# Taking seven more pairs of a gated MLP's hidden states down by block products, with their sums on VectorE

## The chip, the cores and the metric

One core of a Trainium2 chip runs the kernel. The metric is the device time of one execution in microseconds, the median over runs. Of the kernel before there are three runs.

## What is computed

All tensors are fp32. x has 2048 rows of 576. The result mixes two branches by a gate g:

```
g = sigmoid((x * gate_w).sum(-1))
a = linear attention with a softmax feature map on 32 heads of 18, then @ wo
gate, up = x @ W_gate, x @ W_up          # 576 x 4608 each
b = (gate * (gate > 0) * up) @ W_down    # 4608 x 576
out = g * a + (1 - g) * b
```

The attention branch and its projections are the first 350 us or so of the kernel. Everything in this document is about branch b, which is the rest.

## The kernel before

**Precision.** A matmul operand is kept as two parts of a narrower format, a high part (a rounding copy by ScalarE, `high`, `high_h`, `high_w`) and a low part (source minus high part, on VectorE: `low`, `low_h`, `low_w`, `low_w_rows`). A product of two blocks is then three matmuls of 128 x 128 by 512 columns: high x high, high x low, low x high.

**Units.** The 4608 hidden columns are 36 chunks of 128, the 2048 rows two halves of 1024. A unit is one chunk for one half: units 0 to 35 are the first half, 36 to 71 the second. `step(u, j)` (L1328) is one of seven steps j of a unit u. In each, TensorE runs one `product` (L1127), 7 matmuls, into a PSUM bank. The seven products are a block form (seven products where eight would be plain) of gate and up for two blocks of 512 rows. The bank `cx` takes four of them one on top of the other (steps 0, 2, 4 and 6), `ca` two (1 and 5), `cy` one (3). In between, a bank is read: ScalarE copies it out (`copy`, L1298: g1 from `cx` in step 1, u2 from `ca` in step 2, g2 from `cx` in step 3), VectorE adds to these copies (step 4: g1, step 5: u2 from `cx`, step 6: g2 from `ca`), and `gated` (L1295) makes the two hidden states, the second of them in step 0 of the next unit. The next product into a bank waits for the reading before it.

**Pairs.** Two units, 2g and 2g + 1, make pair g: four hidden states e1, e2, o1, o2 of 128 x 512. Pair g is taken down (multiplied by W_down, added to the output `ac` that stays in SBUF) during the two units of pair g + 1: behind each product stand some matmuls of the way down, whose sum VectorE adds to `ac` in the next step (`add_up`, L1279). There are 18 pairs a half (NG). Two ways down exist:
- `down_plain` (L1152), all pairs of the first half: eight blocks of 512 columns, each 6 matmuls and one add, and 8 matmuls for the last 64 of the 576 output columns, 56 matmuls and 8 adds. It needs 4 hidden states split in two and one split of the weights (`plain_down`, L1116).
- `down` (L1186), the second half's pairs but the last: fourteen block products of 3 matmuls and 8 for the last columns, 50 matmuls and 14 adds. It needs more sums: four differences of states (`minus`), 7 split states, and of each half of the weights four sums (`down_sums_of_blocks`, L1084, on GpSimd) and two splits (`prepare_down`, L1313).

**What else a unit does.** In the first half each unit also makes the next unit's gate and up operands from raw weights: high and low parts of three blocks (`blocks`, tile wb), four sums of blocks in place (`sums_of_blocks`, L891, VectorE), high and low parts of these (`block_sums`, tile ws). They are stored to DRAM, and the second half loads them. VectorE also works off 18 operations that prepare x for the second half (`second_half`, tile xb, one a unit from unit 4 on). Down weights come by `load_down` (L915) into one buffer.

**What sets the order.** `in_order` holds each engine's instructions in the order in which the program writes them, that of `step`. Engines meet through semaphores only. So an instruction that waits holds all that stands behind it on its engine. ScalarE's queue mixes the copies of banks with the high parts of states and weights.

Of the kernel before, what the change touches and what calls it, by code (L numbers as in the profile page):

```python
# [19 lines left out]
NC = F // P  # L20
# [63 lines left out]
def gated_mix_kernel(  # L84
# [26 lines left out]
    SUB, ADD, MULT = ALU.subtract, ALU.add, ALU.mult  # L111
    tt, pt = nc.vector.tensor_tensor, nc.gpsimd.tensor_tensor
# [98 lines left out]
    with tc.tile_pool(name="ps_v", bufs=1, space=PSUM) as ps_v:  # L211
# [7 lines left out]
        for k in range(5):  # L219
            w = raw.tile([P, TB + VW], F32, name="xwv", tag="raw")  # L220
# [438 lines left out]
    t = NT - 1  # L659
# [203 lines left out]
    NG = NC // 2  # L863
# [24 lines left out]
            WO[u] = {1: (o, 0), 2: (o, 1), 4: (o, 2)}  # L888
        f(WB[u], RAW[u][:, 0:3])

    def sums_of_blocks(u):  # L891

        a = RAW[u]
        f = tt
        f(out=a[:, 2], in0=a[:, 2], in1=a[:, 3], op=ADD)
        f(out=a[:, 3], in0=a[:, 0], in1=a[:, 3], op=SUB)
        f(out=a[:, 0], in0=a[:, 2], in1=a[:, 0], op=SUB)
        f(out=a[:, 1], in0=a[:, 1], in1=a[:, 0], op=SUB)

    def block_sums(u, f):  # L900
        if u not in WS:
# [163 lines left out]
    WD, W4, HID, ACC, ACC4, BANK, REST = {}, {}, {}, {}, {}, {}, {}  # L1065
# [17 lines left out]

    def down_sums_of_blocks(g, m):  # L1084
        a = down_raw(g, m)
        pt(out=a[:, 2], in0=a[:, 2], in1=a[:, 3], op=ADD)
        pt(out=a[:, 3], in0=a[:, 0], in1=a[:, 3], op=SUB)
        pt(out=a[:, 0], in0=a[:, 2], in1=a[:, 0], op=SUB)
        pt(out=a[:, 1], in0=a[:, 1], in1=a[:, 0], op=SUB)

    def down_block_sums(g, m, f):
        f(WD[g, m][:, :, 3:7], down_raw(g, m))
# [9 lines left out]
    def rest_weights(g, step):  # L1102

        a = WDR[g][:, 8 * P:].rearrange("p (c q) -> p c q", c=2)
        if step == 0:
            nc.scalar.activation(W4[g][:, 0:2, 0], a, AF.Copy)
        elif step == 1:
            tt(out=W4[g][:, 0:2, 1], in0=a, in1=W4[g][:, 0:2, 0].bitcast(F32), op=SUB)
            pt(out=a[:, 0], in0=a[:, 0], in1=a[:, 1], op=ADD)
        elif step == 2:  # L1110
            nc.scalar.activation(W4[g][:, 2, 0], a[:, 0], AF.Copy)
            nc.scalar.activation(W4[g][:, 3], W4[g][:, 1].bitcast(F32), AF.Copy, scale=-1.0)
        else:
            tt(out=W4[g][:, 2, 1], in0=a[:, 0], in1=W4[g][:, 2, 0].bitcast(F32), op=SUB)
# [29 lines left out]
    def load_rest(hf):  # L1144
        for t in range(2):
            a = ACC4[hf, t] = sums_of[t][:64, 2]
            nc.sync.dma_start(a, att[4 * P:, rows(0, 0, t, hf)[1]])

    PLAIN = {1: (0, 0, 1), 2: (0, 1, 1), 3: (2, 0, 1), 4: (0, 0, 0), 5: (0, 1, 0), 6: (2, 0, 0),
             8: (1, 0, 1), 9: (1, 1, 1), 11: (1, 0, 0), 12: (1, 1, 0)}  # L1150

    def down_plain(g, s):  # L1152
# [30 lines left out]
            return []  # L1183
        return add

    def down(g, s, bank):  # L1186

        first, last = g == NG, g == 2 * NG - 2
        m, i = divmod(s, 7)
        n = DOWN[i]  # L1190
        key = 0 if n in (1, 6, 7, 4) else 1
        if n in (1, 5, 2):
            BANK[m, key] = bank(m, n)
        ps = BANK[m, key]
        h, l = HID[g, n]
        o, k = WD[g, m], PLACE[n]
        mm = lambda ps, w, v, a, z: nc.tensor.matmul(ps, w, v, start=a, stop=z, skip_group_check=True)  # L1197
        mm(ps, o[:, 0, k], h, n in (1, 5, 2), False)
        mm(ps, o[:, 0, k], l, False, False)
        mm(ps, o[:, 1, k], h, False, True)  # L1200
        if m == 0 and n in (1, 5, 2, 4):
            w, r = {1: (0, 0), 5: (2, 1), 2: (1, 0), 4: (3, 1)}[n]
            if first and n in (1, 5):
                REST[r] = pm.tile([P, TB], F32, name=f"pm{r}")
            w = W4[g][:, w].rearrange("p s q -> p (s q)")
            mm(REST[r], w, h, first and n in (1, 5), False)
            mm(REST[r], w, l, False, last and n in (2, 4))

        def add():
            i, t = ADDS[n]  # L1210
            a = ACC[1, i, m, t]
            tt(out=a, in0=ps, in1=a, op=ADD)  # L1212
            return []
        return add
# [22 lines left out]
    def high_h(key, src):  # L1237
        h, l = hp.tile([P, TB], F32R, name="hh"), hp.tile([P, TB], F32R, name="hl")
        nc.scalar.activation(h, src, AF.Copy)  # L1239
        HID[key] = h, l  # L1240

    def low_h(key, src):
        h, l = HID[key]
        tt(out=l, in0=src, in1=h.bitcast(F32), op=SUB)  # L1244
# [29 lines left out]
    EVEN, ODD, T, LATE, PEND = {}, {}, {}, [], []  # L1274
# [16 lines left out]
    def minus(a, b):  # L1291

        tt(out=b, in0=a, in1=b, op=SUB)

    def gated(g, up):  # L1295
        nc.vector.scalar_tensor_tensor(out=g, in0=g, scalar=0.0, in1=up, op0=ALU.max, op1=MULT)  # L1296

    def copy(ps, name):  # L1298
        a = tp.tile([P, TB], F32, name=name, tag="tp")
        nc.scalar.activation(a, ps, AF.Copy)  # L1300
        return a
# [26 lines left out]
    def step(u, j):  # L1328


        g, odd = divmod(u, 2)
        v, q = u + 1, g - 1
        plain, was_plain = g < NG or g == 2 * NG - 1, q < NG
        ps, first = bank(SEQ[j])
        product(ps, u, SEQ[j], first)
        add_up()
        make = 0 < u < NC - 1
        cx, ca, cy = (BANKS.get(n) for n in ("cx", "ca", "cy"))
        old = not odd and g > 0

# [9 lines left out]
        if odd and plain or old and was_plain:  # L1350
            key, x2, x1 = ((g, 0), e2, e1) if odd else ((q, 1), o2, o1)
            if j == 0:
                high_h(key + (1,), x2)
            elif j == 1:
                high_h(key + (0,), x1)
                low_h(key + (1,), x2)
            elif j == 2:
                low_h(key + (0,), x1)
        elif odd:
            if j == 1:  # L1360
                high_h((g, 1), e1)
            elif j == 3:
                low_h((g, 1), e1)
                minus(e2, e1)
            elif j == 4:
                high_h((g, 5), e1)
            elif j == 5:
                low_h((g, 5), e1)
        elif old:
            if j == 0:  # L1370
                high_h((q, 6), e1)
                minus(o2, e2)
            elif j == 1:
                high_h((q, 3), o2)
                low_h((q, 6), e1)
            elif j == 2:
                low_h((q, 3), o2)
                high_h((q, 7), e2)
                high_h((q, 2), o1)
            elif j == 3:  # L1380
                minus(o1, e1)
                low_h((q, 7), e2)
            elif j == 4:
                high_h((q, 4), e1)
                low_h((q, 2), o1)
            elif j == 5:
                low_h((q, 4), e1)

        if make:
            if j == 0:  # L1390
                blocks(v, high_w)
                if v + 1 < NC:
                    load_w(v + 1)
            elif j == 1:
                blocks(v, low_w)
                blocks(v, low_w_rows)
            elif j == 2:
                if v < NC - 2:
                    nc.sync.dma_start(wbd[v], WB.pop(v).bitcast(F32))
                sums_of_blocks(v)  # L1400
            elif j == 4:
                if u > 1:
                    block_sums(v, low_w)
                    block_sums(v, low_w_rows)
            elif j == 5:
                if 2 < v < NC - 2:
                    nc.sync.dma_start(wsd[v], WS.pop(v).bitcast(F32))
        elif j == 0 and NC < u < 2 * NC - 1:
            load_operands(v)

        if j == 1:
            T["g1"] = copy(cx, "g1")
        elif j == 2:
            T["u2"] = copy(ca, "u2")
        elif j == 3:
            T["g2"] = copy(cx, "g2")
            if make:
                block_sums(v, high_w)
        elif j == 4:
            tt(out=T["g1"], in0=cy, in1=T["g1"], op=ADD)  # L1420
        elif j == 5:
            tt(out=T["u2"], in0=cx, in1=T["u2"], op=ADD)  # L1422
            if u == 1:
                block_sums(v, low_w)
                block_sums(v, low_w_rows)
                nc.sync.dma_start(wsd[v], WS.pop(v).bitcast(F32))
        elif j == 6:
            a = T["g2"]
            tt(out=a, in0=ca, in1=a, op=ADD)
            gated(a, T["u2"])  # L1430
            if odd and not plain:
                minus(a, e1)
            LATE[:] = [a, (cx, T["g1"])]
            w = WO.pop(u)
            if NC - 2 <= u < NC:
                WO[u + 2] = w
# [7 lines left out]
            prepare_down(g, 0, j)  # L1444
        elif old and not was_plain:
            prepare_down(q, 1, j)
        if old and j == 5:
            load_down(g)
        if old and j == 6:
            ODD.pop(q)  # L1450
# [28 lines left out]
                store_rest(0, 1)  # L1479
                load_rest(1)  # L1480
        if j == 6 and u < NC:
            if u >= 4:
                next(later_half, None)
            if u == NC - 3:
                for _ in later_half:
                    pass
                load_operand(1, 0)
                load_operand(1, 1)
# [157 lines left out]
```

## Time and profile before

| what | value |
|---|---|
| median of 3 runs | 1581.5 us (1580.53 to 1581.55) |
| the profiled execution | 1581.88 us, its span 1579.4 us |
| granted TensorE clock over the span | 1.000 |
| DMA | 283.38 MB, mean 179 GB/s |

The profile is of one execution. Its times count from the span's start. Engines are PE (TensorE), PEld (its weight loads), DVE (VectorE), ACT (ScalarE), POOL (GpSimd) and SP (the engine whose queue issues most DMAs). A record is an instruction's time on its engine; records of one engine can overlap a little, so the distance between two starts is what an instruction takes from the queue.

### The profile page before, as it was taken

What the parts mean: (1) busy time and instruction counts of PE and PEld (TensorE: products, weight loads), DVE (VectorE), ACT (ScalarE), POOL (GpSimd) and SP (SyncE); (2) the same over time, 40 slices, a digit from 0 to 9 for tenths busy, and PEclk for the clock granted to TensorE, in tenths of its full rate; (3) what the DMA queues carried; (4) which work ended last, traced back from release to release, by engine and by line L of the source; (5) the groups of instructions that cost most, each with busy time, mean ns of one, the idle gap of its engine ahead of it and who ended that gap; (6) DMA issues with size and microseconds to landing.
All of it is one profiled execution on the core that took longest, in us unless ns stands there. A gap on an engine that the chain in (4) does not pass through costs nothing.

```text
span 1579.4 us, 20181 instructions
## 1 busy us (share of the span) xinstructions
PE 1568.7 (99%) x7823; PEld 1313.6 (83%) x7823; DVE 1190.2 (75%) x1865; ACT 558.3 (35%) x918; POOL 175.7 (11%) x243
## 2 busy tenths in 40 slices
PE   9999999999999999999999999999999999999998
PEld 9999995678888888888888888888888888888887
DVE  4997776497787777877777777777777777777777
ACT  4354335563333333333333333232222332232321
POOL 0126521110000000000000002111111111111110
PEclk9999999999999999999999999999999999999999
DMA  5365415596755675555545516543443443443432
GB/s 165 105 202 186 167 33 154 180 359 265 257 201 199 221 277 207 192 222 214 196 176 210 220 43 231 196 177 132 158 179 132 166 156 132 179 157 132 186 136 75
DMA packets 64539, 283.38 MB, mean 179 GB/s; under 512 B 6802, under 2 KB 17298, under 8 KB 55740
## 3 DMA queue, kind: packets, MB, share of 16 engines
q1 hardware_dynamic: 61228, 270.34, 47.0%
q0 software_dynamic: 2352, 10.11, 2.0%
q10 hardware_dynamic: 864, 1.65, 0.3%
q8 instruction: 61, 1.00, 0.3%
q14 instruction: 34, 0.28, 0.0%
HBM read 172.07 MB, written 108.60 MB: 178 GB/s over the span
## 4 chain that ended last, share of the span: by engine, by line
PE 95%; DMA 2%; DVE 2%; ACT 1%; issue 0%; POOL 0%; SPq 0%; DVEq 0%; ACTq 0%; POOLq 0%
PE cx L1134 28%; PE ca L1134 14%; PE pd L1174 12%; PE pd L1197 10%; PE cy L1134 7%; PE kv L175 4%; PE pk L175 3%; PE pq L175 3%; PE pm L1174 2%; PE pm L1197 2%; PE kv L421 1%; PE pv L237 1%; PE po L562 1%; PE ptr L379 1%; PE pw L175 1%; PE psf L259 1%
## 5 line engine op out<-in xcount | busy, mean ns | idle before, releaser
L1239 ACT ACTIVATE hh<-g 128x512 fp32r<-128x512 f32 x195 | 120.1, 624 | 456.9 <-DVE g L1296 287.5
L1212 DVE TENSOR_TENSOR ac<-pd,ac 128x512 f32<-128x512 f32 x238 | 164.0, 689 | 144.1 <-PE pd L1197 144.0
L1134 PE MATMUL cx<-xo,ws 128*128 128x512 f32 x1008 | 252.0, 389 | 0.9 <-ACT g L1300 0.9
L1134 PE MATMUL ca<-xo,ws 128*128 128x512 f32 x1008 | 251.9, 389 | 0.0
L1134 PE MATMUL cx<-xo,wb 128*128 128x512 f32 x1008 | 249.0, 389 | 0.1
L1134 PEld LDWEIGHTS cx<-xo,ws 128*128 128x128 f32 x1008 | 189.2, 188 | 40.5 <-ACT g L1300 1.3
L1134 PEld LDWEIGHTS cx<-xo,wb 128*128 128x128 f32 x1008 | 188.2, 188 | 41.0 <-DVE u L1422 0.5
L1134 PEld LDWEIGHTS ca<-xo,ws 128*128 128x128 f32 x1008 | 189.2, 188 | 39.2
L1174 PE MATMUL pd<-hh,wd 128*128 128x512 f32 x576 | 200.7, 389 | 0.0
L1197 PE MATMUL pd<-hh,wd 128*128 128x512 f32 x476 | 185.2, 389 | 0.0
L1180 DVE TENSOR_TENSOR ac<-pd,ac 128x512 f32<-128x512 f32 x144 | 99.1, 688 | 103.8 <-PE pd L1174 103.8
L1244 DVE TENSOR_TENSOR hl<-g,hh 128x512 fp32r<-128x512 f32 x195 | 135.6, 696 | 2.0 <-ACT hh L1239 0.2
L1300 ACT ACTIVATE g<-cx 128x512 f32<-128x512 f32 x144 | 84.9, 590 | 129.4 <-PE cx L1134 129.3
L1174 PEld LDWEIGHTS pd<-hh,wd 128*128 128x128 f32 x576 | 108.1, 188 | 22.5
L1134 PE MATMUL cy<-xo,wb 128*128 128x512 f32 x504 | 125.9, 389 | 0.0
L1097 ACT ACTIVATE wd<-wdr 128x384 fp32r<-128x384 f32 (+1 forms) x106 | 62.3, 606 | 143.3 <-DMA wdr<-wd 143.3
L1174 PE MATMUL pd<-hl,wd 128*128 128x512 f32 x288 | 112.0, 389 | 0.0
L1134 PEld LDWEIGHTS cy<-xo,wb 128*128 128x128 f32 x504 | 94.6, 188 | 19.6
L1197 PEld LDWEIGHTS pd<-hh,wd 128*128 128x128 f32 x476 | 89.4, 188 | 18.5
L1197 PE MATMUL pd<-hl,wd 128*128 128x512 f32 x238 | 92.6, 389 | 0.0
L841 POOL TENSOR_TENSOR xo<-xr,xo 32x512 fp32r<-32x512 f32 x5 | 8.3, 1675 | 614.4 <-ACT xo L857 613.8
L1100 DVE TENSOR_TENSOR wd<-wdr,wd 128x384 fp32r<-128x384 f32 (+1 forms) x106 | 68.7, 663 | 1.4 <-ACT wd L1097 1.4
(256 smaller groups left out, 2562.8 us busy)
## 6 DMA issues: line engine op xcount, KB each, us to landing
wsd<-ws SPq DMA_DIRECT2D x34, 1280.0 KB
ws<-wsd SPq DMA_DIRECT2D x34, 1280.0 KB
wbd<-wb SPq DMA_DIRECT2D x34, 960.0 KB
wb<-wbd SPq DMA_DIRECT2D x34, 960.0 KB
wr<-wgu SPq DMA_DIRECT2D x36, 768.0 KB
wdr<-wd SPq DMA_DIRECT2D x36, 576.0 KB
eT<-et SPq DMA_DIRECT2D x10, 594.0 KB
xt<-xb SPq DMA_DIRECT2D x7, 768.0 KB
```

The costliest lines, as they stand in the source:

```text
L175: nc.tensor.matmul(ps, w, m, start=i == 0, stop=i == len(pairs) - 1)
L237: nc.tensor.matmul(pv[i][c], m, w_[:, k, cs], start=k == 0 and n == 0, stop=k == 4 and n == 1)
L1097: nc.scalar.activation(o[:, 0], a, AF.Copy)
L1100: tt(out=o[:, 1], in0=a, in1=o[:, 0].bitcast(F32), op=SUB)
L1134: nc.tensor.matmul(ps, w, v, start=first and m == 0, stop=m == len(pairs) - 1, skip_group_check=True)
L1174: nc.tensor.matmul(ps, w, v, start=k == 0 and (i < 2 or first), stop=k == len(mms) - 1 and (i < 2 or last), skip_group_check=True)
L1180: tt(out=a, in0=ps, in1=a, op=ADD)
L1197: mm = lambda ps, w, v, a, z: nc.tensor.matmul(ps, w, v, start=a, stop=z, skip_group_check=True)
L1212: tt(out=a, in0=ps, in1=a, op=ADD)
L1239: nc.scalar.activation(h, src, AF.Copy)
L1244: tt(out=l, in0=src, in1=h.bitcast(F32), op=SUB)
L1300: nc.scalar.activation(a, ps, AF.Copy)
```

## The change

Pairs 3, 5, 7, 9, 11, 13 and 15 of the first half (`BY_BLOCKS`) go down by `down` in place of `down_plain`. For these:
- the sums of down weights are made on VectorE, and the last columns use the plain weights with unsummed states, for which state e2 is split too (key 8), so two of the four steps of `rest_weights` fall away;
- while such a pair is taken down (`heavy`), ScalarE copies bank `cx` out in step 5 (x7) and VectorE adds u2 from the copy in step 6; two of the four sums of weight blocks move from step 2 to step 3, and the low parts of ws from step 4 to step 5;
- a difference and a high part of the states move ahead by one or two steps, the down weights of such a pair are loaded in step 1 in place of 5, and the even heavy unit leaves out its operation on xb.

```diff
         f(WB[u], RAW[u][:, 0:3])
-    def sums_of_blocks(u):
+    def sums_of_blocks(u, part=None):
         a = RAW[u]
-        f = tt
-        f(out=a[:, 2], in0=a[:, 2], in1=a[:, 3], op=ADD)
-        f(out=a[:, 3], in0=a[:, 0], in1=a[:, 3], op=SUB)
-        f(out=a[:, 0], in0=a[:, 2], in1=a[:, 0], op=SUB)
-        f(out=a[:, 1], in0=a[:, 1], in1=a[:, 0], op=SUB)
+        if part != 1:
+            tt(out=a[:, 2], in0=a[:, 2], in1=a[:, 3], op=ADD)
+            tt(out=a[:, 3], in0=a[:, 0], in1=a[:, 3], op=SUB)
+        if part != 0:
+            tt(out=a[:, 0], in0=a[:, 2], in1=a[:, 0], op=SUB)
+            tt(out=a[:, 1], in0=a[:, 1], in1=a[:, 0], op=SUB)
...
         a = down_raw(g, m)
-        pt(out=a[:, 2], in0=a[:, 2], in1=a[:, 3], op=ADD)
-        pt(out=a[:, 3], in0=a[:, 0], in1=a[:, 3], op=SUB)
-        pt(out=a[:, 0], in0=a[:, 2], in1=a[:, 0], op=SUB)
-        pt(out=a[:, 1], in0=a[:, 1], in1=a[:, 0], op=SUB)
+        f = tt if g < NG else pt
+        f(out=a[:, 2], in0=a[:, 2], in1=a[:, 3], op=ADD)
+        f(out=a[:, 3], in0=a[:, 0], in1=a[:, 3], op=SUB)
+        f(out=a[:, 0], in0=a[:, 2], in1=a[:, 0], op=SUB)
+        f(out=a[:, 1], in0=a[:, 1], in1=a[:, 0], op=SUB)
...
             tt(out=W4[g][:, 0:2, 1], in0=a, in1=W4[g][:, 0:2, 0].bitcast(F32), op=SUB)
-            pt(out=a[:, 0], in0=a[:, 0], in1=a[:, 1], op=ADD)
+            if g >= NG:
+                pt(out=a[:, 0], in0=a[:, 0], in1=a[:, 1], op=ADD)
+        elif g < NG:
+            return
...
             nc.sync.dma_start(a, att[4 * P:, rows(0, 0, t, hf)[1]])
+
+    BY_BLOCKS = range(3, NG - 2, 2)
+
+    def is_plain(g):
+        return g < NG and g not in BY_BLOCKS or g == 2 * NG - 1
...
         return add
+    REST_OF = ({1: (0, 0, 1), 5: (0, 1, 8), 3: (1, 1, 3), 2: (1, 0, 2)},
+               {1: (0, 0, 1), 5: (2, 1, 5), 2: (1, 0, 2), 4: (3, 1, 4)})
+
...
         mm(ps, o[:, 1, k], h, False, True)
-        if m == 0 and n in (1, 5, 2, 4):
-            w, r = {1: (0, 0), 5: (2, 1), 2: (1, 0), 4: (3, 1)}[n]
+        rest = REST_OF[g // NG]
+        if m == 0 and n in rest:
+            w, r, i = rest[n]
+            h, l = HID[g, i]
...
             i, t = ADDS[n]
-            a = ACC[1, i, m, t]
+            a = ACC[g // NG, i, m, t]
...
         v, q = u + 1, g - 1
-        plain, was_plain = g < NG or g == 2 * NG - 1, q < NG
+        plain, was_plain = is_plain(g), is_plain(q)
...
         make = 0 < u < NC - 1
+        heavy = q in BY_BLOCKS
...
         elif odd:
+            if g < NG and j < 2:
+                (high_h, low_h)[j]((g, 8), e2)
...
                 low_h((q, 6), e1)
+                if heavy:
+                    minus(o1, e1)
...
             elif j == 3:
-                minus(o1, e1)
+                if not heavy:
+                    minus(o1, e1)
                 low_h((q, 7), e2)
+                if heavy:
+                    high_h((q, 4), e1)
             elif j == 4:
-                high_h((q, 4), e1)
+                if not heavy:
+                    high_h((q, 4), e1)
...
                     nc.sync.dma_start(wbd[v], WB.pop(v).bitcast(F32))
-                sums_of_blocks(v)
+                sums_of_blocks(v, 0 if heavy else None)
+            elif j == 3:
+                if heavy:
+                    sums_of_blocks(v, 1)
             elif j == 4:
-                if u > 1:
+                if u > 1 and not heavy:
...
             elif j == 5:
-                if 2 < v < NC - 2:
+                if 2 < v < NC - 2 and not heavy:
...
         elif j == 5:
-            tt(out=T["u2"], in0=cx, in1=T["u2"], op=ADD)
-            if u == 1:
+            if heavy:
+                T["x7"] = copy(cx, "x7")
+            else:
+                tt(out=T["u2"], in0=cx, in1=T["u2"], op=ADD)
+            if u == 1 or heavy:
...
             tt(out=a, in0=ca, in1=a, op=ADD)
+            if heavy:
+                tt(out=T["u2"], in0=T["x7"], in1=T["u2"], op=ADD)
...
             prepare_down(q, 1, j)
-        if old and j == 5:
+        if old and j == (1 if was_plain and not plain else 5):
...
         if j == 6 and u < NC:
-            if u >= 4:
+            if u >= 4 and not (old and q in BY_BLOCKS):
...
```

How it moves instructions is seen at two places. Names: `ac` is the output, `pd` a bank of the way down, `hl` and `hh` a state's low and high part, `g` a state or a bank's copy, `wr`, `wb`, `ws` the raw and split gate and up weights, `wdr`, `wd` the raw and split down weights.

VectorE in steps 1 to 3 of unit 12, in which pair 5 is taken down and pair 6 begun. Before:

```order
L1180 TENSOR_TENSOR ac<-pd_5186,ac 128x512
L1244 TENSOR_TENSOR hl<-g_5058,hh 128x512
L895 TENSOR_TENSOR wr<-wr 128x384
L896 TENSOR_TENSOR wr<-wr 128x384
L897 TENSOR_TENSOR wr<-wr 128x384
L898 TENSOR_TENSOR wr<-wr 128x384
L1180 TENSOR_TENSOR ac<-pd_5209,ac 128x512
```

Now:

```order
L1227 TENSOR_TENSOR ac<-pd_5245,ac 128x512
L1259 TENSOR_TENSOR hl<-g_5144,hh 128x512
L895 TENSOR_TENSOR wr<-wr 128x384
L896 TENSOR_TENSOR wr<-wr 128x384
L1088 TENSOR_TENSOR wdr<-wdr 128x128
L1089 TENSOR_TENSOR wdr<-wdr 128x128
L1090 TENSOR_TENSOR wdr<-wdr 128x128
L1091 TENSOR_TENSOR wdr<-wdr 128x128
L1227 TENSOR_TENSOR ac<-pd_5220,ac 128x512
L1259 TENSOR_TENSOR hl<-g_5005,hh 128x512
L898 TENSOR_TENSOR wr<-wr 128x384
L899 TENSOR_TENSOR wr<-wr 128x384
```

Between two adds now stand the sums of down weights, and two of the four sums of gate and up weights have moved behind the second add and one more low part.

ScalarE from the last steps of unit 12 to step 1 of unit 13 (the last row is the copy of `cx` that unit 13's third product waits for). Before:

```order
L874 ACTIVATE ws<-wr 128x4x384
L1239 ACTIVATE hh<-g_5225 128x512
L874 ACTIVATE wb<-wr 128x3x384
L1239 ACTIVATE hh<-g_5184 128x512
L1300 ACTIVATE g_5315<-cx 128x512
```

Now:

```order
L874 ACTIVATE ws<-wr 128x4x384
L1099 ACTIVATE wd<-wdr 128x512
L1315 ACTIVATE x_5325<-cx 128x512
L1254 ACTIVATE hh<-g_5293 128x512
L874 ACTIVATE wb<-wr 128x3x384
L1254 ACTIVATE hh<-g_5242 128x512
L1315 ACTIVATE g_5389<-cx 128x512
```

A high part of down weights and the new copy x stand ahead; the four rows up to the copy of `cx` are in the same order as before. Over the whole program TensorE has 42 matmuls fewer, VectorE 175 operations more, ScalarE 63 more, and GpSimd the same.

## Rows read from the trace of the kernel before

**Rows 1.** The page, part 1: busy time, share of the span, instructions.
```profile
PE 1568.7 (99%) x7823; PEld 1313.6 (83%) x7823; DVE 1190.2 (75%) x1865; ACT 558.3 (35%) x918; POOL 175.7 (11%) x243
```

**Rows 2.** Busy time by stretch: an even and an odd unit of the first half.
```profile
core 0: us, PE busy (x) PEld busy (x) DVE busy (x) ACT busy (x) POOL busy (x), PEclk, DMA share, GB/s
643.13:660.59 17.46, 17.46 (x79) 14.46 (x78) 13.40 (x22) 5.38 (x8) 0.00 (x0) 1.00 0.60 219
660.59:678.04 17.45, 17.45 (x79) 14.45 (x78) 14.54 (x24) 6.53 (x10) 0.00 (x0) 1.00 0.57 214
```

**Rows 3.** Timeline of TensorE: start, us, engine, line, operation, out<-in, count.
```profile
646.02 0.39 PE L1174 MATMUL pd<-hh,wd 128*128 128x512 f32 x1
646.25 1.75 PE L1134 MATMUL cx<-xo,ws 128*128 128x512 f32 x7
647.84 0.39 PE L1174 MATMUL pd<-hh,wd 128*128 128x512 f32 x1
```

**Rows 4.** Timeline of VectorE, columns as in rows 3, idle time before in brackets.
```profile
646.45 0.69 DVE L1180 TENSOR_TENSOR ac<-pd,ac 128x512 f32<-128x512 f32 x1 [0.60 <-PE pd L1174]
647.06 0.68 DVE L1244 TENSOR_TENSOR hl<-g,hh 128x512 fp32r<-128x512 f32 x1
647.66 0.55 DVE L895 TENSOR_TENSOR wr<-wr 128x384 f32<-128x384 f32 x1
648.25 0.56 DVE L896 TENSOR_TENSOR wr<-wr 128x384 f32<-128x384 f32 x1
...
649.43 0.56 DVE L898 TENSOR_TENSOR wr<-wr 128x384 f32<-128x384 f32 x1
649.91 0.68 DVE L1180 TENSOR_TENSOR ac<-pd,ac 128x512 f32<-128x512 f32 x1
...
659.72 0.95 DVE L341 TENSOR_TENSOR xb<-xb 128x768 f32<-128x768 f32 x1
660.59 0.68 DVE L1296 SCALAR_TENSOR_TENSOR g<-g,cx 128x512 f32<-128x512 f32 x1
...
661.78 0.95 DVE L877 TENSOR_TENSOR wb<-wr,wb 128x768 fp32r<-128x768 f32 x1
662.75 0.55 DVE L880 TENSOR_TENSOR wb<-wr,wb 32x384 fp32r<-32x384 f32 x1
...
670.20 1.22 DVE L877 TENSOR_TENSOR ws<-wr,ws 128x1024 fp32r<-128x1024 f32 x1
671.43 0.68 DVE L880 TENSOR_TENSOR ws<-wr,ws 32x512 fp32r<-32x512 f32 x1
672.15 0.69 DVE L1420 TENSOR_TENSOR g<-cy,g 128x512 f32<-128x512 f32 x1
```

**Rows 5.** Timeline of ScalarE at the start of an odd unit.
```profile
659.83 0.63 ACT L1239 ACTIVATE hh<-g 128x512 fp32r<-128x512 f32 x1 [8.32 <-DVE g L1296]
660.37 1.15 ACT L874 ACTIVATE wb<-wr 128x1152 fp32r<-128x1152 f32 x1
661.42 0.61 ACT L1239 ACTIVATE hh<-g 128x512 fp32r<-128x512 f32 x1
661.95 0.58 ACT L1300 ACTIVATE g<-cx 128x512 f32<-128x512 f32 x1
```

**Rows 6.** Timeline of all engines in the first half's second unit.
```profile
352.16 1.17 ACT L874 ACTIVATE wb<-wr 128x1152 fp32r<-128x1152 f32 x1 [1.70 <-DMA wbd<-wb]
...
353.75 0.58 ACT L1300 ACTIVATE g<-cx 128x512 f32<-128x512 f32 x1
...
354.38 1.89 PE L1134 MATMUL cx<-xo,ws 128*128 128x512 f32 x7 [0.87 <-ACT g L1300]
...
356.11 1.76 PE L1134 MATMUL cy<-xo,wb 128*128 128x512 f32 x7
```

**Rows 7.** Groups by form: VectorE at 128 columns, GpSimd's first sum of down weights.
```profile
L1100 DVE TENSOR_TENSOR wd<-wdr,wd 128x128 fp32r<-128x128 f32 x19 | 5.4, 282 | 0.0
L1086 POOL TENSOR_TENSOR wdr<-wdr 128x128 f32<-128x128 f32 x34 | 15.7, 463 | 239.9 <-DVE wd L1100 239.9
```

**Rows 8.** The page, part 5: ScalarE's high parts of the down weights.
```profile
L1097 ACT ACTIVATE wd<-wdr 128x384 fp32r<-128x384 f32 (+1 forms) x106 | 62.3, 606 | 143.3 <-DMA wdr<-wd 143.3
```

## The prediction

> **What bounds the kernel now.** I read the page's shares first: TensorE is busy 99% of the span, VectorE 75%, ScalarE 35% [rows 1]. Then the busy time of one even and one odd unit of the first half: TensorE fills both stretches, VectorE works 13.40 us of the even 17.46 us and 14.54 us of the odd 17.45 us, so 27.94 us of a pair's 34.91 us, and the granted clock is 1.00 [rows 2]. Then the pitch of a matmul: seven of them start within 1.59 us, 0.227 us each [rows 3]. A pair has 98 product matmuls and 56 of the way down, 154 x 0.227 = 34.9 us: the stretch is nothing but matmuls without a gap. Last I looked at the place where another engine has held TensorE in this same loop, for that is what a saving on TensorE can turn into. There is one: ScalarE waits 1.70 us with the weights' high parts, does a state's high part behind them, and only then copies the gate's bank out; the third product of the unit, which accumulates into that bank, starts 0.05 us after the copy's end, with TensorE idle for 0.87 us before it [rows 6]. The first seven matmuls after such a wait take 1.73 us in place of 1.59 us, so a restart costs 0.14 us.
>
> **What the change takes from TensorE.** A pair that goes down by blocks needs 14 products of 3 matmuls and 4 x 2 for the last 64 columns, 50 in place of 56. Seven pairs: 42 x 0.227 = 9.5 us less. Nothing is added there.
>
> **What it puts on VectorE.** Prices are taken from one start to the next, since the records overlap [rows 4]: 0.61 us for an add out of PSUM, 0.60 us for a low part of 512 columns, 0.58 us for a 384-column sum whose successor waits for it and 0.48 us for one that nobody waits for (so waiting for the operation just ahead costs 0.11 us, and I take 0.71 us for 512 columns), 0.97 us and 1.23 us for the low parts of the two weight tiles, 0.72 us for the 32-row part behind the second (0.59 us by the same for the smaller one, whose record lasts 0.55 us), 0.87 us for one operation on the second half's sums xb. A 128-column operation lasts 0.28 us on VectorE [rows 7]; in a chain I take 0.32 us, and 0.20 us for the last. The second half's sums of down weights last 0.46 us on GpSimd [rows 7], which does nothing in these stretches [rows 2].
>
> By two pairs (four units), VectorE gets 6 more adds (3.7 us), 4 more low parts of states (2.4 us), 4 differences (2.6 us with their waits), 8 sums of down weights (2.3 us) and 1.0 us more of down weights' low parts: 12.0 us on 55.9 us, less 0.9 us for the xb operation that the third unit now skips. That is 67.0 us, against 302 x 0.227 = 68.5 us of matmuls. VectorE is then level with TensorE over four units, with no room for order. And the load isn't even. Call A the even and B the odd unit in which a by-block pair is made, C and D the two in which it is taken down. TensorE has 81, 73, 78 and 70 matmuls there, 18.4, 16.5, 17.7 and 15.9 us; VectorE about 13.4, 17.7, 19.5 and 16.5 us. It loses time to TensorE in B, C and D, and gets it back in A.
>
> **Where that ends.** The wait is worked out from the last place in B where VectorE waits for TensorE, the add of B's second step, to the copy that D's third product waits for.
> - VectorE: from that add to the start of D's first gate operation (on C's second gate bank) stand 55 operations: 10 adds (6.1), 16 of 512 columns (9.6), 5 more whose successor waits (3.6), 8 sums of 384 (4.35), 1 of 384 (0.5), 8 sums of 128 (2.3), one small weight tile's low parts (1.55), two large ones' (3.9), one xb (0.87): 32.8 us, all back to back, since each one's operands are there before it.
> - Then ScalarE, in its own order [rows 5]: the gate takes 0.69 us, the high part 0.54 us, the weights' high parts 1.05 us, the next high part 0.53 us, the gate bank's copy 0.58 us; with a handover of 0.05 us at either end [rows 6] 3.5 us.
> - TensorE: from the group of matmuls after the one that released the first add (VectorE starts 0.2 us behind it [rows 3, 4]) to D's third product stand 151 matmuls, 34.2 us.
>
> So the copy ends at 0.2 + 32.8 + 3.5 = 36.5 us where TensorE is ready at 34.2 us: 2.2 us late, and 2.35 us with the restart. Which waits share it is open (part of it should fall on C's last product, which now waits for the bank copied out by ScalarE); their sum is not. In A VectorE has 5 us to spare, so nothing is carried on to the next group. Of the seven groups four have the xb operation in B and three don't (1.48 us): 4 x 2.35 + 3 x 1.48 = 13.8 us.
>
> **A price weighed.** Behind a 512-column operation the next starts after 0.60 us, though its record lasts 0.68 us [rows 4]. The Trainium skill, "VectorE: DVE Perf Modes", section "The DRAIN you can't avoid", says that the next operation does not start until the pipe has emptied; by that the 26 free-standing operations of 512 columns would take 0.08 us more each, the copy would be 2.1 us later still, and the time some 15 us higher. The rows show starts inside the record, so I price by starts.
>
> **What costs nothing.** The 14 copies of a bank by ScalarE (0.58 us each) and 49 more state and weight high parts lie on an engine that is 35% busy, as long as it isn't behind VectorE; where it is, they are in the chain above. The load of a by-block pair's down weights is issued four steps earlier, into a buffer that the plain pair before has left. The low parts of the large weight tile move one step back, with two steps still ahead of their first product. SP's stores move with them. If that cover goes, the third rival prices it.
>
> **Sum.** The profiled execution took 1581.9 us (span 1579.4 us and 2.5 us around it), 0.4 us over the median. 1581.9 - 9.5 + 13.8 = 1586.2 us, against the median's run **1585.8 us**. An error of 1% in VectorE's 32.8 us is 0.33 us a group, 2.3 us in all, so this case alone reaches from 1583 to 1589 us.
>
> **Rivals.**
> - **The full gain** (the other side, faster): VectorE's lag stays inside the buffers and TensorE keeps its pace: 1581.5 - 9.5 = 1572 us. For it: 75% on the page looks like room; the Trainium skill, "Perfetto Trace Analysis", section "Identifying the Most-Contended Engine", would have the engine of the highest occupancy relieved first, which is what the change does. It decides at 2.2 us of the 36.5 us: the waits for the operation just ahead (16 x 0.11 us) and the draining around 32-row operations (0.6 us) together make that much, and if neither counted under load, nothing would be late. Against: every such pair of rows in the trace pays them [rows 4]. Chance 0.15.
> - **A draw**: the lateness is half as large, because operations move ahead of each other's waits or the copy's chain is shorter; 1.36 us a group just eats the 9.5 us: 1581.5 us, and 1578 to 1584 us around it. Chance 0.30, with the lower end of my own case.
> - **More waits behind ScalarE**: the plain pair's down weights are loaded in C only after VectorE's late low part, and behind the store of a large weight tile; ScalarE takes them up in D's third step, ahead of the copy of the second gate bank. In the second half ScalarE does wait for this load, 143.3 us in 17 times, 8.4 us each [rows 8], there without harm. Each us of it that TensorE sees is 7 us: up to 1593 us. Chance 0.10.
> - My forecast, VectorE as the bound over three units of four: chance 0.45.
>
> A measurement of this kernel can tell about 0.2% from no change, 3.2 us. Slower by more is above 1584.7 us: the forecast's case but for its lower end, and the third rival, 0.53. Within: 0.30. Faster: 0.17. The range leaves out most of the full gain and the end of the third rival: 1577 to 1592 us.
>
> **What would show it.** In the changed kernel's profile TensorE should have 42 matmuls fewer, and idle time in front of the third product of unit D, ended by ScalarE's copy of the gate bank, 1 to 2 us seven times; VectorE should run B to D without a gap, its share near 80%, and A should still show it idle. The second half must be as before. It is wrong if TensorE shows no idle time in the by-block units (full gain), if VectorE idles in C, or if TensorE waits at a place that hangs on a DMA.

## The result and the profile after

The changed kernel takes 1584.7 us (median of 17 runs, 1582.95 to 1588.8) against 1580.2 us for the kernel before in 17 runs beside it (1578.24 to 1582.95): a ratio of 1.0028 with a 95% interval of 1.0021 to 1.0034; the medians differ by 4.5 us. The prediction was 4.3 us slower than the median that stood before it, with slower the likeliest case.

Shares of the span on the page of the changed kernel, then the chain that ended last and two groups of TensorE's matmuls, with the idle time before them behind the second bar:

```profile
PE 1567.7 (99%) x7781; PEld 1304.4 (82%) x7781; DVE 1266.7 (80%) x2040; ACT 585.1 (37%) x981; POOL 175.1 (11%) x243
...
PE 83%; DVE 12%; DMA 2%; ACT 1%; issue 1%; POOL 0%; SPq 0%; ACTq 0%; DVEq 0%; POOLq 0%
...
L1139 PE MATMUL cx<-xo,ws 128*128 128x512 f32 x1008 | 253.3, 390 | 6.9 <-ACT g L1315 6.8
L1139 PE MATMUL cx<-xo,wb 128*128 128x512 f32 x1008 | 251.7, 391 | 1.1 <-ACT x L1315 0.2
```

Against [rows 1] TensorE has 42 matmuls fewer, VectorE 175 operations more and 80% in place of 75%. TensorE's share is 99% as before, so the shares alone show no loss. The chain does: 12% of it now runs on VectorE, 2% before the change, and ahead of products into the bank `cx` TensorE is idle for 6.8 us in total, waiting for ScalarE's copy of the gate's bank. From the waits of the changed kernel's TensorE (total, times, longest, us):

```profile
PE cx L1139 <- ACT g L1315: 6.8, 7, 1.1
```

Seven times, once for each pair taken down by blocks: 1.1 us four times and 0.8 us three times, by the starts. This view covers the whole program; in some runs below it also counts, under the same name, the wait of the first half's second unit [rows 6], which has nothing to do with the change. Where the seven are shows in one group of four units, 10 to 13, called A, B, C and D as in the prediction. Busy time in four stretches, each from VectorE's last gate operation for the unit before to that for the unit itself, columns as in [rows 2]:

```profile
508.70:525.10 16.40, 16.40 (x74) 13.37 (x73) 13.45 (x22) 4.84 (x8) 0.00 (x0) 1.00 0.82 293
525.10:543.70 18.60, 18.53 (x82) 15.04 (x81) 17.48 (x31) 7.08 (x12) 0.00 (x0) 1.00 0.49 181
543.70:563.30 19.60, 19.45 (x85) 15.59 (x85) 19.27 (x35) 8.04 (x13) 0.00 (x0) 1.00 0.36 138
563.30:579.60 16.30, 15.19 (x67) 12.21 (x66) 16.11 (x26) 7.72 (x12) 0.00 (x0) 1.00 0.61 237
```

VectorE is idle for 2.95 us in A, 1.1 us in B, 0.3 us in C and 0.2 us in D, where it was idle for 4.1 us and 2.9 us in the units of [rows 2]. GpSimd does nothing, and the granted clock stays 1.00. TensorE's timeline of the same group: A's second product (into `ca`), the two products that were late, and the second product of the next A.

```profile
507.71 1.75 PE L1139 MATMUL ca<-xo,ws 128*128 128x512 f32 x7
...
557.31 1.88 PE L1139 MATMUL cx<-xo,wb 128*128 128x512 f32 x7 [0.15 <-ACT x L1315]
...
565.53 1.88 PE L1139 MATMUL cx<-xo,ws 128*128 128x512 f32 x7 [1.11 <-ACT g L1315]
...
578.58 1.75 PE L1139 MATMUL ca<-xo,ws 128*128 128x512 f32 x7
```

From the first row to the last are 70.87 us and 302 matmuls, a group's whole number. At the pitch of [rows 3], 0.227 us, these take 68.55 us, so the group is 2.3 us late. The losses stand at C's last product (it waits for the new copy x) and at D's third (it waits for the gate bank's copy). A smaller one, by the starts 0.2 us and a restart, stands at B's last product, behind VectorE's u2.

ScalarE at D's start:

```profile
562.79 0.63 ACT L1254 ACTIVATE hh<-g 128x512 fp32r<-128x512 f32 x1 [5.53 <-DVE g L1311]
563.33 1.15 ACT L874 ACTIVATE wb<-wr 128x1152 fp32r<-128x1152 f32 x1
564.38 0.61 ACT L1254 ACTIVATE hh<-g 128x512 fp32r<-128x512 f32 x1
564.90 0.58 ACT L1315 ACTIVATE g<-cx 128x512 f32<-128x512 f32 x1
...
566.72 1.06 ACT L1099 ACTIVATE wd<-wdr 128x1024 fp32r<-128x1024 f32 x1 [0.76 <-DMA wdr<-wd]
```

These are the same four operations with the same durations as [rows 5]. ScalarE had nothing to do for 5.53 us before them: it waited for VectorE's gate. The copy ends at 565.48 and TensorE starts at 565.53. VectorE, from the add in B's second step on, and just ahead of that gate (the row at 562.06):

```profile
529.30 0.69 DVE L1190 TENSOR_TENSOR ac<-pd,ac 128x512 f32<-128x512 f32 x1 [0.71 <-PE pd L1184]
...
560.15 0.68 DVE L1227 TENSOR_TENSOR ac<-pd,ac 128x512 f32<-128x512 f32 x1
560.75 0.68 DVE L1459 TENSOR_TENSOR g<-ca,g 128x512 f32<-128x512 f32 x1
561.35 0.68 DVE L1461 TENSOR_TENSOR u<-x,u 128x512 f32<-128x512 f32 x1
562.06 0.69 DVE L1311 SCALAR_TENSOR_TENSOR g<-g,u 128x512 f32<-128x512 f32 x1
562.67 0.68 DVE L1227 TENSOR_TENSOR ac<-pd,ac 128x512 f32<-128x512 f32 x1
```

Starts follow each other by 0.60 us, or 0.71 us where an operation waits for the one ahead (561.35 to 562.06), as in [rows 4]. The first row is the last for which VectorE waits in this group. Behind it no row has idle time in brackets: from 529.30 to 562.06 it starts 55 operations in 32.76 us. All four groups with an xb operation in B take 32.7 to 32.8 us for this run of operations, the three without (54 operations) 31.9 us.

Over the whole program: from the first matmul of unit 6 to that of unit 36, where all seven pairs lie, the kernel before takes 523.6 us and the changed one 528.3 us. From there to the end of the last matmul both take 619.0 us. The stage ahead of unit 6 took 429 to 435 us in the profiled executions of this study, whatever was changed behind it. The changed kernel's profiled execution was its longest run (1588.8 us), so its span stands 7.6 us over the one before where the medians differ by 4.5 us; the experiments are therefore also compared by the stretch from unit 6 to unit 36, here called the loop.

### The profile page after: what moved, and what is told of

It reads as the page before. It is cut to its first block, busy times and chain, and to the rows that moved or that the text cites. A ratio compares the mean times of both kernels' runs of the same rounds, so it can differ in the third digit from the quotient of the medians.

```text
span 1587.0 us, 20327 instructions
## 1 busy us (share of the span) xinstructions
PE 1567.7 (99%) x7781; PEld 1304.4 (82%) x7781; DVE 1266.7 (80%) x2040; ACT 585.1 (37%) x981; POOL 175.1 (11%) x243
## 4 chain that ended last, share of the span: by engine, by line
PE 83%; DVE 12%; DMA 2%; ACT 1%; issue 1%; POOL 0%; SPq 0%; ACTq 0%; DVEq 0%; POOLq 0%
PE cx L1139 25%; PE pd L1210 13%; PE ca L1139 12%; PE cy L1139 6%; PE pd L1184 6%; PE kv L175 4%; PE pk L175 3%; PE pq L175 3%; PE pm L1210 2%; DVE hl L1259 1%; PE pm L1184 1%; PE kv L421 1%; PE pv L237 1%; DVE ac L1190 1%; DVE ac L1227 1%
## 5 line engine op out<-in xcount | busy, mean ns | idle before, releaser
L1227 DVE TENSOR_TENSOR ac<-pd,ac 128x512 f32<-128x512 f32 x336 | 230.9, 687 | 144.8 <-PE pd L1210 144.2
L1254 ACT ACTIVATE hh<-g 128x512 fp32r<-128x512 f32 x223 | 136.8, 624 | 429.1 <-DVE g L1308 223.8
L1259 DVE TENSOR_TENSOR hl<-g,hh 128x512 fp32r<-128x512 f32 x223 | 154.2, 691 | 0.8 <-ACT hh L1254 0.2
L1210 PEld LDWEIGHTS pd<-hh,wd 128*128 128x128 f32 x672 | 126.1, 188 | 26.3
L1210 PE MATMUL pd<-hl,wd 128*128 128x512 f32 x336 | 131.0, 390 | 0.0
L1099 ACT ACTIVATE wd<-wdr 128x384 fp32r<-128x384 f32 (+1 forms) x120 | 69.4, 588 | 137.4 <-DMA wdr<-wd 137.4
L1190 DVE TENSOR_TENSOR ac<-pd,ac 128x512 f32<-128x512 f32 x88 | 60.5, 687 | 43.1 <-PE pd L1184 42.4
L874 ACT ACTIVATE ws<-wr 128x1536 fp32r<-128x1536 f32 x36 | 53.7, 1490 | 76.8 <-DVE wr L899 76.8
L1184 PEld LDWEIGHTS pd<-hh,wd 128*128 128x128 f32 x352 | 66.1, 188 | 13.7
L1102 DVE TENSOR_TENSOR wd<-wdr,wd 128x384 fp32r<-128x384 f32 (+1 forms) x120 | 76.3, 644 | 0.7
```

The lines of the kernel that those rows point to most:

```text
L874: nc.scalar.activation(o[:, :, 0:3], a, AF.Copy)
L1099: nc.scalar.activation(o[:, 0], a, AF.Copy)
L1102: tt(out=o[:, 1], in0=a, in1=o[:, 0].bitcast(F32), op=SUB)
L1184: nc.tensor.matmul(ps, w, v, start=k == 0 and (i < 2 or first), stop=k == len(mms) - 1 and (i < 2 or last), skip_group_check=True)
```

## The experiments

The theory: VectorE, back to back from B to D, is what TensorE waits for, and each us of work taken out of that run is worth 1 us a group. The rivals: it is the order of ScalarE's queue; it is VectorE's load over all four units, wherever the work stands; it is the new copy x7.

**One: the sums of down weights on GpSimd again.** 

```diff
-        f = tt if g < NG else pt
+        f = pt
```

> One part of the change undone: the sums of the by-block pairs' down weights go back to GpSimd. Theory (VectorE's work from unit B's second step to unit D's first gate decides when the gate bank is copied, 2.1 us late): both sets of four sums, 2.3 us, leave that run, so TensorE waits 0 to 0.6 us a group in place of 1.4 to 2.1 us; the 9.5 us saved remain but for 0 to 4 us: ratio to the kernel before 0.994 to 0.9965. Rival 1 (ScalarE's own queue, not VectorE's work, makes the copy late): as the change, 1.003. Rival 2 (GpSimd's sums take longer in a row, 2.0 us against 1.2 us, and then hold ScalarE's high parts of the down weights): a new wait of about 0.8 us a group, 0.998.

1575.3 us, ratio to before 0.9971 (0.9962 to 0.9981), a little above the range that was expected; loop 519.6 us, 8.7 us under the changed kernel. The eight sums a group were the price: without them the change gains. TensorE's wait for the gate bank's copy falls from 6.8 us to this:

```profile
PE cx L1139 <- ACT g L1315: 3.7, 5, 0.8
```

One of the five, 0.5 us, is that of the first half's second unit; the other four, 0.8 us each, are those of the groups with an xb operation in B. ScalarE waits nowhere in the loop for GpSimd's sums, so the expectation's second rival falls. A group got 1.2 us shorter, not the 2.3 us that the sums take, and the trace shows where the rest went. VectorE is now early enough in B to wait 0.46 us for TensorE there, so that much of the saving is idle time; and its own 384-column sums take 0.56 us more a group, since VectorE and GpSimd slow each other. GpSimd's timeline in one group of this kernel:

```profile
472.54 0.46 POOL L1088 TENSOR_TENSOR wdr<-wdr 128x128 f32<-128x128 f32 x1 [17.78 <-DVE wd L1102]
473.08 0.90 POOL L1089 TENSOR_TENSOR wdr<-wdr 128x128 f32<-128x128 f32 x1
474.06 0.66 POOL L1090 TENSOR_TENSOR wdr<-wdr 128x128 f32<-128x128 f32 x1
474.80 0.65 POOL L1091 TENSOR_TENSOR wdr<-wdr 128x128 f32<-128x128 f32 x1
```

and VectorE's beside it:

```profile
472.98 0.68 DVE L1259 TENSOR_TENSOR hl<-g,hh 128x512 fp32r<-128x512 f32 x1
473.58 0.82 DVE L895 TENSOR_TENSOR wr<-wr 128x384 f32<-128x384 f32 x1
474.43 0.70 DVE L896 TENSOR_TENSOR wr<-wr 128x384 f32<-128x384 f32 x1
475.06 0.68 DVE L1227 TENSOR_TENSOR ac<-pd,ac 128x512 f32<-128x512 f32 x1
```

The 384-column sum takes 0.82 us in place of 0.55 us [rows 4], GpSimd's 0.90 us in place of 0.46 us [rows 7]. The first of GpSimd's sums, beside an add that reads PSUM, keeps its 0.46 us, and the add out of PSUM beside the last one its 0.68 us. Nor does every operation pay: the low part (first row), beside which GpSimd's slowest sum starts, keeps its 0.68 us. The Trainium skill, "SBUF — State Buffer", section "Who interferes with whom", says that a VectorE instruction with two SBUF inputs contends with a GpSimd instruction that reads SBUF; the slowed sums of either engine agree with it.

**Two: the gate bank's copy first in ScalarE's queue.** In D it moves to step 0, ahead of both high parts of states and that of wb.

```diff
+        if j == 0 and heavy and odd:
+            T["g1"] = copy(cx, "g1")
...
-            T["g1"] = copy(cx, "g1")
+            if not (heavy and odd):
+                T["g1"] = copy(cx, "g1")
```

> In unit D alone, ScalarE copies the gate bank in step 0, ahead of the high parts that wait for VectorE, in place of step 1. Theory (VectorE is the bound over B, C and D): the wait at D's third product goes, and the lag shows at the next place that hangs on VectorE (a bank of the way down, the copy or the add a unit later): between 0 and 5 us less than the change, ratio 1.000 to 1.003. Rival (ScalarE's order is the cause, VectorE's lag alone is harmless): the 1.1 to 1.4 us in front of D's third product go in all seven groups, 9 us less: 0.997.

1583.2 us, ratio 1.0023 (1.0014 to 1.0033); loop 527.6 us, 0.7 us under the changed kernel. The wait at D's third product goes, and comes back a unit later. From TensorE's waits:

```profile
PE pd L1184 <- DVE ac L1227: 3.4, 5, 0.7
```

It is the way down of the next A that waits there, behind five of the seven groups, for VectorE's add to leave its bank; behind the other two, the next even unit's own third product waits, 0.2 us each. ScalarE's order decides where the wait stands and not how long it is, and the first rival falls.

**Three and four: the same extra work in B, and in A.** Both repeat the low part of a state twice, which adds two VectorE operations to a group and changes nothing computed. The first edit is in the odd unit B at step 3, the second in the even unit A at step 2.

```diff
+            if g < NG and j == 3:
+                low_h((g, 8), e2)
+                low_h((g, 8), e2)
```

```diff
+                if old and g in BY_BLOCKS:
+                    low_h(key + (0,), x1)
+                    low_h(key + (0,), x1)
```

> Two operations of 512 columns more on VectorE in unit B's fourth step (a low part made three times over). Theory: 1.2 us more in the run in each of seven groups, all of it seen by TensorE, 8.4 us more than the change: ratio 1.008. Rival (the waits are of fixed size, from the order of the queues, and VectorE has room): as the change, 1.003.

> The same two operations more, but in unit A's third step, which lies outside the run. Theory: A has 2.9 us of idle time on VectorE to take the 1.2 us; as the change, ratio 1.003. Rival (VectorE is the bound over all four units, so that any work added anywhere counts): 8.4 us more, 1.008.

In B: 1592.9 us, ratio 1.0086 (1.0073 to 1.01); loop 537.8 us, 9.5 us over the changed kernel; by the medians, each against the kernel before beside it, 8.7 us. VectorE's run from B's second step to the gate grew from 32.76 us to 34.09 us, 1.33 us for the two operations where 1.2 us were expected. Seven times that is 9.3 us, so all of it is paid. TensorE now waits most at B's last product:

```profile
PE cx L1139 <- DVE u L1455: 9.8, 7, 1.4
PE cx L1139 <- ACT g L1315: 7.3, 8, 1.1
```

The waits at D's third product stay (the eighth of the second row, 0.4 us, is that of the first half's second unit).

In A: 1583.8 us, ratio 1.0027 (1.0017 to 1.0037); loop 528.5 us, no change. Its waits have the same row as the changed kernel, 6.8 us in 7 times. The same work costs everything in one unit and nothing in the other, and the second rival falls: VectorE's total over the four units isn't the bound.

**Five: the copy x7 undone.** VectorE reads the bank itself in step 5, as before the change.

```diff
-            if heavy:
-                T["x7"] = copy(cx, "x7")
-            else:
-                tt(out=T["u2"], in0=cx, in1=T["u2"], op=ADD)
+            tt(out=T["u2"], in0=cx, in1=T["u2"], op=ADD)
...
-            if heavy:
-                tt(out=T["u2"], in0=T["x7"], in1=T["u2"], op=ADD)
```

> One part of the change undone: VectorE reads bank cx itself in step 5 again, no copy x7 by ScalarE. Theory (the run's length on VectorE sets the sum of the waits, not the place where they show): the wait in front of C's last product grows from 0.4 us to about 1.6 us with its restart, the one in front of D's third product shrinks by as much; as the change, ratio 1.002 to 1.0035. Rival (the copy by ScalarE is worth its place: without it a wait of its own comes on top): 1.2 us a group more, 1.008.

1583.7 us, ratio 1.003 (1.0019 to 1.0041); loop 528.6 us. The wait moves to the product that needs this bank, and its sum stays:

```profile
PE cx L1139 <- DVE u L1449: 5.8, 7, 1.2
...
PE cx L1139 <- ACT g L1315: 1.0, 4, 0.5
```

Half of the last row is again that of the first half's second unit. So the third rival falls too: ScalarE's copy neither costs nor gives anything here. It hands on a lag that is VectorE's.

**Six: the xb operation out of B,** with two in A in its place.

```diff
-            if u >= 4 and not (old and q in BY_BLOCKS):
+            if u >= 4 and g not in BY_BLOCKS and not (old and heavy):
+                next(later_half, None)
+            elif old and g in BY_BLOCKS:
+                next(later_half, None)
                 next(later_half, None)
```

> The changed kernel with the operation on xb taken out of unit B (four groups have one) and two in unit A in place of one. Theory: the four groups with an xb operation come to the 1.4 us of the three without, 4 x 0.7 us less: ratio 1.001. Rival (VectorE is the bound over all four units): as the change, 1.003.

1581.7 us, ratio 1.0014 (1.0005 to 1.0023); loop 525.4 us. That is 2.5 us less than the changed kernel by the medians, each against the kernel before beside it, and 2.8 us by the loop (528.26 to 525.43 us), where four groups without their 0.87 us give 3.5 us. The four groups come from 2.2 to 2.4 us late to 1.5 to 1.7 us, near the 1.4 us of the three that never had the operation.

**Seven: one and six together.**

> Sums of down weights on GpSimd and the xb operation out of unit B, both. Theory: with the sums on GpSimd four groups still wait 0.95 us and three 0.08 us; without the xb operation all wait at most 0.1 us, and nearly the whole 9.5 us is left: ratio 0.994 to 0.9955. Rival (GpSimd's sums and VectorE's operations hold each other where they overlap, and A, now fuller, hands on its lag): 0.997 as with the sums alone.

1572.7 us, ratio 0.9954 (0.994 to 0.9968); loop 516.2 us. That is 7.4 us under the loop before, of the 9.5 us that the 42 matmuls take: 0.3 us a group is still lost. Most of it stands where it stood. D's third product in the group of units 10 to 13, with the matmuls beside it, and ScalarE's copy of the gate bank ahead of it:

```profile
557.94 0.58 ACT L1315 ACTIVATE g<-cx 128x512 f32<-128x512 f32 x1
...
558.26 0.39 PE L1210 MATMUL pd<-hh,wd 128*128 128x512 f32 x1
558.57 1.89 PE L1139 MATMUL cx<-xo,ws 128*128 128x512 f32 x7
560.29 0.39 PE L1210 MATMUL pd<-hh,wd 128*128 128x512 f32 x1
```

The copy still ends 0.05 us ahead of the product's start, as in [rows 6]. The product starts 0.31 us behind the matmul before it in place of 0.227 us, and its seven matmuls take 1.72 us in place of 1.59 us. That is 0.21 us, the same in all seven groups, 1.5 of the 2.1 us.

**Eight: as seven, and pair 1 by blocks as well.**

```diff
-    BY_BLOCKS = range(3, NG - 2, 2)
+    BY_BLOCKS = range(1, NG - 2, 2)
```

> As the one before with pair 1 by blocks too, eight pairs. Theory: six matmuls less, 1.36 us, and no wait in its group: 0.9935. Rival (at the start of the first half the loads of raw weights and the operations on x still hold ScalarE and VectorE): no gain over seven pairs or a loss, 0.995 to 0.997.

1574.8 us, ratio 0.9973 (0.9962 to 0.9983), a miss: 2.1 us slower than seven, although six more matmuls (1.4 us) are gone. The loads of xb are steps of the same list as its operations; two of these in one step put a load and its first operation together, and VectorE waits for the DMA, in front of the operations that TensorE needs:

```profile
379.82 0.96 DVE L335 TENSOR_TENSOR xb<-xb,ac 128x768 f32<-128x768 f32 x1 [1.69 <-DMA xb<-xs]
...
588.35 0.96 DVE L335 TENSOR_TENSOR xb<-xb,ac 128x768 f32<-128x768 f32 x1 [3.01 <-DMA xb<-xs]
```

**Nine and ten: eight pairs, with A's two xb operations two steps apart, at `j` of 4 and 6, and none ahead of unit 4; and the kernel of seven once more beside it.**

```diff
+        if j == 4 and 4 <= u < NC and old and g in BY_BLOCKS:
+            next(later_half, None)
...
+            elif u >= 4 and old and g in BY_BLOCKS:
                 next(later_half, None)
```

> Eight pairs by blocks as before, but unit A's two operations on xb stand in two different steps (5 and 7), and none before unit 4. In the run before, VectorE waited 3.0 us and 1.7 us for the load of xb where the load and its first operation stood in one step, and TensorE lost about 2.3 us behind that. Theory: these waits go, 2.3 us less than the eight pairs before, 1.2 us less than the seven: ratio 0.994 to 0.9955. Rival (the eighth pair itself costs more than its six matmuls, at the start of the half): 0.996 to 0.997.

> The seven pairs with sums on GpSimd and xb out of B once more, on the same chip as the eight, to compare the two. Theory: 1.2 us above the eight pairs; ratio 0.9945 to 0.9965.

Eight pairs: 1570.8 us, ratio 0.994 (0.9926 to 0.9953), the lowest median here and 9.5 us under the kernel before. Seven pairs: 1571.8 us, 0.9949 (0.9936 to 0.9961). The stall is mended. The two times differ by 1.0 us and their intervals overlap, but the traces show the eighth pair's own group: from the first matmul of unit 2 to that of unit 6 eight pairs take 68.67 us and seven 69.81 us, so the pair is worth 1.1 of its six matmuls' 1.4 us.

## Why the prediction was right

- **TensorE's gain**, 9.5 us, was as forecast in matmuls, and at the pitch of [rows 3] outside the waits.
- **VectorE's loss**, 13.8 us in the sum: the loop got 4.6 us longer (523.62 to 528.26 us) with 9.5 us of matmuls less, so 14.2 us were lost. Group by group, at the pitch of [rows 3], the four with an xb operation in B are 2.2 to 2.4 us late and the three without 1.35 to 1.45 us, where the terms were 2.35 and 1.48 us. The size is not luck: the run of 55 operations was put at 32.8 us and took 32.76 us, and ScalarE's chain behind it, put at 3.5 us with its handovers, took 3.47 us (562.06 to 565.53). The row read as 0.58 us for a 384-column sum is 0.59 us in [rows 4], which changes nothing. Runs three, four and six bear out the mechanism: the price of an operation in B to D is its distance to the next start, and in A it is zero.
- **Its place** was left open between two waits; it stands at both, and at a third that wasn't named (B's last product). At D's third product TensorE is idle for 1.1 or 0.8 us, where 1 to 2 us were named. Runs two and five show why that doesn't matter: the wait moves, its sum doesn't.
- **A's spare time** was put at 5 us. TensorE's unit A takes 18.45 us (its first product starts at 506.12 us, B's at 524.57 us) and VectorE works 13.45 us: about 2 us of the difference go into catching up, and 2.95 us are idle. So no lag reaches the next group.
- **The weighed price.** By the Trainium skill's rule on draining ("VectorE: DVE Perf Modes"), the time would have come out some 15 us higher; the loaded run still starts an operation of 512 columns 0.60 us after the one before, so the rows were the right price. The rule was read by half there: the same section says that a next operation that is not held starts earlier, and the trace agrees with that.
- **The full gain** did not come: VectorE at 80% on the page is back to back from B's second step to D. The Trainium skill's rule to relieve the most occupied engine first ("Perfetto Trace Analysis", "Identifying the Most-Contended Engine") names TensorE here, also by the weight loads' busy share that the section asks for (83% against VectorE's 75% [rows 1]). Relieving it at VectorE's cost made the kernel slower, and relieving VectorE (run one) made the changed kernel 9.0 us faster with no matmul less, each against the kernel before beside it.
- **The draw** fails by the size: it needed 1.36 us a group, and 1.9 us came on average (13.5 us in seven groups).
- **More waits behind ScalarE**: ScalarE did wait for the plain pair's down weights, 0.76 us in the row at 566.72, but behind the gate bank's copy. The copy of the second gate bank, which stands behind these high parts, ended at 568.46 us, and the product that needs it started at 570.19 us, without idle time before it, so nothing of the wait was seen.

What stays open is the rest of what run seven still loses, 0.6 us in all, beside the 1.5 us at D's third product; by the starts most of it stands at A's third.

## What to carry to other kernels

A saving on the engine that bounds a loop is worth only as much as the next engine can follow, and that is read unit by unit: count the operations that must follow each other without a gap between two handovers, at start-to-start prices, against the bound engine's work between the same two. When such a run is too long, another order or another engine to read the bank only moves the wait; work has to leave the run, to an engine or a unit that is idle. A filler operation that is moved must keep its distance from its own load, or the cure brings a new wait.

## What was unexpected

VectorE and GpSimd slowed each other when both summed tiles in SBUF: at most, 0.55 us became 0.82 us on VectorE and 0.46 us became 0.90 us on GpSimd, while an add that reads PSUM kept its 0.68 us. Moving eight sums a group was still worth 9.0 us by the medians and 8.7 us by the loop. Nor did the clock fall in the idle gap of 1.1 us on TensorE: it was granted at 1.00 in all four stretches shown, 2.4 GHz.
